# Windowed attention into a GEGLU feed-forward on one core: the first batch's loads, masks and order of work rearranged, and the second batch's attention moved into the first output stage

## The chip, the core and the metric

The kernel runs on one core of a Trainium2 chip. The core has a matrix engine (PE, which reads its stationary operand with separate weight loads, PEld), a vector engine (DVE), a scalar engine (ACT), a general-purpose engine (POOL) and SP, which here only issues transfers. Each engine works through its own list of instructions in order; they meet at semaphores. Transfers between main memory and the on-chip memory (SBUF) are issued from SP, ACT or POOL and are carried by 16 DMA engines. In this kernel the transfers that POOL issues for q, k, v and the weights convert 32-bit to 16-bit floating point on the way; they are called cast DMAs here. Matmul results go to PSUM, eight banks of 512 32-bit columns in each of 128 partitions.

The metric is the device time of one execution in microseconds (us). Lower is better.

## The reference, cut to what matters

```python
batch, n_heads, seq, head_dim = (8, 8, 576, 64)      # q, k, v, f32
window, dilation, scale = 32, 4, 1 / 8
rel = pos[:, None] - pos[None, :]
mask_plain = (rel >= 0) & (rel < window)
mask_dil = (rel >= 0) & (rel < window * dilation) & (rel % dilation == 0)
# heads 0-3 use mask_plain, heads 4-7 use mask_dil
attn = softmax(where(mask, scale * q @ k.T, -1e9))
x = (attn @ v).transpose(0, 2, 1, 3).reshape(4608, 512)
g, val = x @ w_gate, x @ w_val                        # 512 x 1536 each
out = (gelu(g) * val) @ w_out                         # 1536 x 512
```

Inputs and output are 32-bit; the kernel computes its matmuls in 16-bit floating point and accumulates in 32 bits.

## The kernel before, in words

**Attention.** Work is cut into pairs of heads, numbered n = 4 b + pair for batch b: two plain pairs and two dilated pairs in each batch (numbers 0 and 1 of batch 0 are plain, 2 and 3 dilated; 4 and 5 plain, 6 and 7 dilated for batch 1). A dilated head is treated as four residue classes of 144 positions, each with a plain window of 32. For each pair `emit_s` makes the scores of only those 128-key blocks that the window touches, in four PSUM banks, and ACT takes their exp into a tile `P`. The mask is applied in one of two ways: with `pe_mask`, a matmul of the identity with a bias of 0 or -60000 is accumulated ahead of the scores; without it, `emit_s` returns a function, called later, which multiplies `P` by a 0/1 mask on DVE (L383). `emit_pv` makes the denominators (`den`, a matmul with ones) and the numerators (`num`, a matmul with V). `norm_r` transposes the denominators out of PSUM into `dt` on DVE, and `recip` takes the reciprocal and transposes back, giving `rb`; `norm_x` multiplies the numerators by `rb` into `xT`, the transposed input of the feed-forward part. `b0` names the first PSUM bank that a step uses.

**Transposed q and k.** For batches 0 and 1 q and k are transposed by PE with an identity matrix. Plain heads come six rows to a partition (`sixes`, 96 partitions), are cast to 16 bits and transposed in `t_plain`; DVE or ACT copies the result out of PSUM into `qTp`. Dilated heads come four rows to a partition (`quads`): 128 partitions for the first 512 rows (`t_dil`) and 16 partitions for the last 64 rows (`t_rest`), copied into `qTd`. Later batches use transposes by DMA.

**Feed-forward.** Tokens go in nine chunks of 512. Per chunk c there are twelve blocks of 128 hidden columns: `ffn1` makes the gate and the value (4 matmuls each), `geglu` takes gelu on ACT (L584) and multiplies on DVE (L585) into `u_all`. Then `ffn2`, the output stage, makes four tiles of 128 tokens, twelve matmuls each (L596), and `store` copies each tile out and sends it away on SP. The first two blocks of chunks 0 and 1 are made together, one quarter of the contraction at a time (`ffn1_two`), so that they can begin when only the first quarter of `xT` is there.

**Order of the work.** The order is written out by hand: instructions stand on each engine in the order of the source. The front (L618 to L686) does batch 0: SP and ACT load plain q and k in 32 bits, then dilated q and k (L622 to L624), then V; POOL loads the identity and the masks from constants in main memory. DVE, ACT and POOL cast. Then scores, denominators and numerators of pairs 0 to 3 follow; pairs 2 and 3 use the banks of their forerunners (`emit_s(2, 0)`, `emit_s(3, 0)`). POOL issues gate and value weights of thirds 0, 1 and 2 by cast DMA (`load_w`, L654, L657, L658); thirds 0, 1, 2 serve blocks 0-3, 4-7, 8-11.

Behind the front (L689 to L708) stand the loads of batch 1: plain q and k on SP, held back until value weights 1 are there (`gate["dma"]`); dilated q and k, then output weights 0 on POOL; four casts of plain q and k; output weights 1 and 2; and then V of batch 1. Batch 1 is transposed between the blocks of chunk 0: a dilated group behind blocks 8 and 11, a plain group behind blocks 9 and 10 (L761 to L767). Output stage 0 (L787 to L799) makes its four tiles one after another, each with the full twelve matmuls, and the scores, denominators and numerators of pairs 4 to 7 are hung between these matmuls as hooks. Every later output stage does the same for the next batch with a list of places; that part is not touched.

Scratch: plain q and k of batch 0 land in the space of `u_all` (`first_p`), dilated q and k in the unused end of `xT` (`first_d`, `first_r`).

## Time and profile before

| | |
|---|---|
| median of 3 runs | 357.31 us (357.14 to 357.68) |
| the profiled execution | 357.14 us, with a span of 355.3 us from its first to its last instruction |
| mean granted clock of PE | 0.986 |
| first FFN matmul | 26.04 us after the start of the span |
| first output matmul | 50.47 us |
| first FFN matmul of chunk 1 | 68.05 us |
| gate weights 0 and value weights 0 issued | 15.84 and 16.61 us; they took 6.9 and 8.6 us to land |
| plain q and k of batch 1 issued | 31.08 and 31.45 us; cast by POOL from 38.96 to 44.3 us |

All times in a profile are counted from the start of the span. The page gives the busy time of each engine, the span in 40 slices of about 8.9 us with the granted clock of PE and the share of the DMA engines, the chain of work that ended last, and groups of like instructions. A table by stage can be asked for any stretch, and the instructions can be listed in order of time. A row of that list reads: start, length, engine, line of the source, operation, what it writes and reads, shape, how many were merged; in brackets the idle time of the engine before it and what ended that. Matmul ends are modelled; in a dense stream one of 512 columns starts every 0.215 us.

### The profile page before, as it was taken

How to read it: one execution, taken by the hardware profiler on the slowest of the kernel's cores; microseconds unless marked ns; L12 is line 12 of the kernel's file. 1: busy time of each engine (PE TensorE's matmuls, PEld its weight loads, DVE VectorE, ACT ScalarE, POOL GpSimd, SP SyncE). 2: the span in 40 equal slices, each digit the busy share in tenths (PEclk: the TensorE clock that was granted, in tenths of full speed). 3: DMA queues.
4: the chain of work that ended last, by engine and by line, in shares of the span. 5: the costliest groups of instructions: out<-in, count | busy, mean ns of one | idle time of the engine just before them, and what ended most of it. 6: DMA issues, size and time to landing. Idle time of an engine off the chain costs nothing.

```text
span 355.3 us, 5974 instructions
## 1 busy us (share of the span) xinstructions
PE 340.1 (96%) x2330; PEld 165.3 (47%) x2330; DVE 202.5 (57%) x313; ACT 146.6 (41%) x217; POOL 78.2 (22%) x110
## 2 busy tenths in 40 slices
PE   5789999999999999999999999999999999999995
PEld 2554454444454444444545454544454444444442
DVE  3575456743486348783778765985399423303420
ACT  2733255253553355535562447236733223323320
POOL 2680334550422350063004500240000000000000
PEclk9959999999999999999999999999999999999999
DMA  8999999999999898799149942792200020020002
GB/s 205 237 176 211 230 151 202 178 165 246 181 140 210 194 165 163 169 163 146 65 135 194 151 93 90 178 156 55 89 2 0 31 89 1 2 89 30 2 30 89
DMA packets 107292, 45.31 MB, mean 128 GB/s; under 512 B 83040, under 2 KB 102496, under 8 KB 107264
## 3 DMA queue, kind: packets, MB, share of 16 engines
q1 hardware_dynamic: 84272, 31.21, 39.5%
q0 software_dynamic: 21456, 12.01, 27.0%
q10 hardware_dynamic: 1536, 1.70, 2.1%
q8 instruction: 18, 0.29, 0.4%
q14 instruction: 10, 0.08, 0.1%
HBM read 40.13 MB, written 9.44 MB: 140 GB/s over the span
## 4 chain that ended last, share of the span: by engine, by line
PE 78%; DVE 13%; DMA 3%; issue 3%; ACT 2%; ACTq 0%; DVEq 0%
PE ps L562 46%; PE ps L596 22%; PE ps L455 5%; DMA xT<-in_k_dram 3%; DVE rb L522 2%; DVE dt L513 2%; DVE dt L483 2%; DVE u_all L585 2%; DVE xT L537 2%; DVE P L383 1%; PE ps L373 1%; DVE xT L493 1%; PE ps L343 1%; DVE rc L520 1%; PE ps L359 1%
## 5 line engine op out<-in xcount | busy, mean ns | idle before, releaser
L585 DVE SCALAR_TENSOR_TENSOR u_all<-g,ps 128x512 f16<-128x512 f16 x108 | 72.7, 683 | 76.8 <-PE ps L562 68.4
L562 PE MATMUL ps<-xT,wg 128*128 128x512 f16 x432 | 114.7, 381 | 0.6 <-DVE xT L534 0.2
L562 PE MATMUL ps<-xT,wv 128*128 128x512 f16 x432 | 114.3, 380 | 0.5 <-ACT osb L607 0.3
L584 ACT ACTIVATE g<-ps 128x512 f16<-128x512 f32 x108 | 63.8, 597 | 121.6 <-PE ps L562 121.5
L596 PE MATMUL ps<-wo,u_all 128*128 128x512 f16 x432 | 100.2, 380 | 0.0
L562 PEld LDWEIGHTS <-wv 128*128 128x128 f16 x432 | 42.4, 98 | 52.4 <-issue 2.5
L562 PEld LDWEIGHTS <-wg 128*128 128x128 f16 x432 | 41.3, 98 | 49.2 <-issue 2.5
L596 PEld LDWEIGHTS <-u_all 128*128 128x128 f16 x432 | 39.4, 98 | 45.2 <-issue 0.2
L607 ACT ACTIVATE osb<-ps 128x512 f32<-128x512 f32 x33 | 19.7, 598 | 38.1 <-PE ps L596 37.5
L199 POOL CAST qp<-st 128x2048 f16<-128x2048 f32 x6 | 11.4, 1894 | 97.6 <-DMA st<-in_k_dram 97.6
L513 DVE STREAM_TRANSPOSE dt<-ps 128x576 f32<-128x576 f32 x23 | 17.9, 779 | 15.4 <-PE ps L455 15.3
L522 DVE STREAM_TRANSPOSE rb<-rc 128x576 f32<-128x576 f32 (+4 forms) x34 | 25.3, 743 | 1.2
L375 ACT ACTIVATE P<-ps 128x1152 f16<-128x1152 f32 x16 | 18.1, 1130 | 18.5 <-PE ps L373 18.5
L353 ACT ACTIVATE P<-ps 128x960 f16<-128x960 f32 x16 | 15.5, 970 | 10.9 <-PE ps L343 10.8
L537 DVE TENSOR_TENSOR xT<-ps,rb 128x576 f16<-128x576 f32 x16 | 17.9, 1130 | 0.3
L609 DVE TENSOR_SCALAR osb<-ps 128x512 f32<-128x512 f32 x3 | 2.1, 691 | 27.8 <-PE ps L596 27.8
L455 PE MATMUL ps<-P,ones 128*64 128x96 f16 (+5 forms) x174 | 12.0, 251 | 4.3 <-DVE P L383 2.1
L383 DVE TENSOR_TENSOR P<-P,mask_p 128x1344 f16<-128x1344 f16 x14 | 12.5, 904 | 5.0 <-ACT P L354 4.9
L455 PEld LDWEIGHTS <-ones 128*64 128x64 f16 x174 | 7.8, 110 | 13.7 <-issue 11.0
L383 DVE TENSOR_TENSOR P<-P,mask_d 128x1152 f16<-128x1152 f16 x11 | 8.3, 757 | 10.2 <-ACT P L375 10.2
L483 DVE STREAM_TRANSPOSE dt<-ps 64x576 f32<-64x576 f32 x14 | 10.9, 781 | 0.4
L183 POOL CAST vp<-sv 128x1024 f16<-128x1024 f32 x8 | 8.5, 1059 | 12.0 <-DMA sv<-in_v_dram 12.0
(83 smaller groups left out, 242.3 us busy)
## 6 DMA issues: line engine op xcount, KB each, us to landing
out_dram<-osb SPq DMA_DIRECT2D x36, 256.0 KB, 2.0
sv<-in_v_dram SPq DMA_DIRECT2D x40, 128.0 KB, 3.9
st<-in_q_dram SPq DMA_DIRECT2D x24, 128.0 KB, 3.4
st<-in_k_dram SPq DMA_DIRECT2D x24, 128.0 KB, 3.0
qd<-in_q_dram POOLq DMA_DIRECT2D x7, 256.0 KB, 5.1
qd<-in_k_dram POOLq DMA_DIRECT2D x7, 256.0 KB, 6.5
vd<-in_v_dram POOLq DMA_DIRECT2D x7, 256.0 KB, 6.8
wg<-in_moe_w_gate_dram POOLq DMA_DIRECT2D x3, 512.0 KB, 7.9
```

What stands on the lines that cost most here:

```text
L375: nc.scalar.activation(pt, ps[:, b0 : b0 + 4, 0:DW], AF.Exp, bias=0.0, scale=scale)
L383: nc.vector.tensor_tensor(pt, pt, mb, ALU.mult)
L455: nc.tensor.matmul(o, lhs, rhs, start=st, stop=True, skip_group_check=True)
L483: nc.vector.transpose(dt[64 * hl : 64 * hl + 64].rearrange("p b c -> p (b c)"), both_rows(1 - hl, b0, hl))
L513: nc.vector.transpose(dst, den)
L522: nc.vector.transpose(rb[:, 0 : 32 * nb].rearrange("p (b c) -> p b c", c=32), bass.AP(tensor=rc.tensor, offset=rc.offset, ap=[rc.ap[0], [1 ...
L537: nc.vector.tensor_tensor(dst.rearrange("p (i m s) -> p i m s", m=2, s=2), num, rb.rearrange("p (s m i) -> p i m s", s=2, m=2), ALU.mult,)
L562: nc.tensor.matmul(ps[:, bank, :], w[:, kc, ns], xT[kc][:, tok], start=first, stop=end)
L584: nc.scalar.activation(g, ps[:, banks[0], :], AF.Gelu)
L585: nc.vector.scalar_tensor_tensor(u_all[:, nb, :], g, USCALE, ps[:, banks[1], :], ALU.mult, ALU.mult)
L596: nc.tensor.matmul(ps[:, bank, :], u_all[:, fc, tb * P : (tb + 1) * P], wo_t[fc // 4][:, fc % 4, :], start=(fc == 0), stop=(fc == NNB - 1),)
L607: nc.scalar.activation(osb, ps[:, bank, :], AF.Copy, bias=0.0, scale=1.0 / USCALE)
```

## The change

In the front:

- Dilated q and k of batch 0 are no longer loaded in 32 bits on SP and ACT. POOL issues them first of all, as cast DMAs, eight rows to a partition (`eights`, 72 partitions). `t_dil` now makes 16 transposes of 72 columns for each half and copies each group of four heads' classes in one piece; `t_rest`, its 32-bit identity and the four 32-bit tiles are gone.
- The identity and both masks are made on POOL with memsets and `affine_select` in place of being loaded. The bias of the plain mask is made on DVE at that place, ahead of the memsets of V and the casts of q; that of the dilated mask moves from POOL to DVE.
- 22 warm-up matmuls in place of 16.
- On POOL the cast of V stands ahead of the first gate and value weights; half of `last_keys` and the cast of dilated V follow before the other weights.
- Pairs 2 and 3 use different banks, so the scores of 3 do not wait for the exp of 2. The denominators of 0 and 1 are taken in a row into scratch of their own. The numerators of 0 and 1 are copied out by ACT and multiplied by POOL (`num_split`).

Behind the front:

- Plain q and k of batch 1 are held until gate weights 2 are there. Dilated q and k of batch 1 (as `eights`) and all of V go ahead of output weights 0 to 2; V's plain part is held until dilated k is there.
- The plain groups of batch 1 are transposed behind blocks 10 and 11, both dilated groups behind the last block. Then scores 4, 5 and 6 and the denominators and numerators of 4 come before any output matmul.
- Output stage 0 works by thirds: the four tiles accumulate in four banks (6, 7, 4, 5), four matmuls each per third, with the rest of the attention of batch 1 between the thirds. A one-column gelu stands at its end.

```diff
@@ front: helpers @@
-    first_d = [x32[t][:, 0 : HK * 4 * D] for t in range(2)]
-    first_r = [x32[2 + t][0:16, 0 : HK * 4 * D] for t in range(2)]
+    first_n = [x32[g][:, 0:S] for g in range(2)]
+    first_t = [x32[2 + g][:, 0:S] for g in range(2)]
+    def identity():
+        nc.gpsimd.memset(ident, 1.0)
+        for sign in (1, -1):
+            nc.gpsimd.affine_select(
+                out=ident, in_=ident, pattern=[[sign, P]], compare_op=ALU.is_ge, fill=0.0, base=0, channel_multiplier=-sign
+            )
+    def band(t, step, off):
+        for sign, base in ((1, off), (-1, WIN - 1 - off)):
+            nc.gpsimd.affine_select(
+                out=t,
+                in_=t,
+                pattern=[[sign * step, t.shape[1]], [sign, t.shape[2]]],
...
+    def mask_plain():
+        nc.gpsimd.memset(mask_p, 1.0)
+        band(mask_p[:, 0:PB].rearrange("p (r c) -> p r c", c=PW), 0, 0)
+        band(mask_p[:, PB : PB + P].rearrange("p (r c) -> p r c", r=1), 0, 0)
+        band(mask_p[:, PB + P : PH].rearrange("p (r c) -> p r c", r=1), 0, 64)
+        nc.vector.tensor_scalar(bias_p, mask_p, 1.0, 60000.0, ALU.subtract, ALU.mult)
+    def mask_dil():
+        nc.gpsimd.memset(mask_d, 1.0)
+        by_class = mask_d.rearrange("p (m i) -> p m i", m=2)
+        band(by_class[:, :, 0:P], 0, 0)
+        band(by_class[:, :, P:NCL], 64, 48)
+    def load_eights(b):
+        q8 = ldp.tile([R8, 2, HK, 8, D], F16, tag="qd", name=f"qd{b}")
+        for t, src in ((0, q), (1, k)):
+            tiles["last"] = nc.gpsimd.dma_start(
+                out=q8[:, t].rearrange("p h r d -> p h (r d)"), in_=eights(src, b, HK, H)
+            )
+        return q8
+    def t_dil(b, hp, q8, b0, engs):
+        qtd_ = tiles["qT", b][1]
+        for t in range(2):
             for hl in range(2):
+                for r in range(4):
+                    c0 = ((hl * 2 + r % 2) * 2 + r // 2) * R8
                     nc.tensor.transpose(
+                        ps16[:, b0 + t, c0 : c0 + R8],
+                        q8[:, t, 2 * hp + hl, 2 * r : 2 * r + 2, :].rearrange("p r d -> p (r d)"),
+                        ident[0:R8, 0:R8],
                     )
             copy(
                 engs[t],
+                qtd_[:, t, 2 * hp : 2 * hp + 2].rearrange("p h m (i u) -> p (h m) i u", u=2),
+                ps16[:, b0 + t, 0:S].rearrange("p (c u i) -> p c i u", c=4, u=2),
+            )
@@ front: order @@
-    nc.gpsimd.dma_start(ident, id_dram.ap())
-    nc.gpsimd.dma_start(mask_p, mp_dram.ap())
-    for t, src, eng in ((0, q, nc.sync), (1, k, nc.scalar)):
-        eng.dma_start(out=fh(first_d[t]), in_=quads(src, 0, HK, 0, 4 * P))
-        eng.dma_start(out=fh(first_r[t]), in_=quads(src, 0, HK, 4 * P, S))
-    nc.gpsimd.dma_start(ident32, id32_dram.ap())
-    nc.gpsimd.dma_start(mask_d, md_dram.ap())
+    qd0 = load_eights(0)
+    identity()
+    mask_plain()
+    mask_dil()
...
-    warm(16, 7)
+    warm(22, 7)
...
+    nc.vector.tensor_scalar(bias_d, mask_d, 1.0, 60000.0, ALU.subtract, ALU.mult)
     load_v_dil_rest(0)
+    v_cast(0, sv0)
     load_w(0)
-    v_cast(0, sv0)
-    copy("pool", tiles["v", 0][1], r4(first_vd))
-    w1 = load_w(1)
-    load_w(2)
...
+    def num_split(n, b0):
+        emit_pv(n, b0, ("num",))
+        rb = tiles.pop(("rb", n))
+        nc.scalar.copy(first_n[n], psf[:, b0 * 512 : b0 * 512 + S])
+        nc.gpsimd.tensor_tensor(xT[n][:, 0:S], first_n[n], rb, ALU.mult)
     emit_s(0, 4, pe_mask=True)
     emit_s(1, 0, pe_mask=True)
...
+    t_dil(0, 0, qd0, 4, ("dve", "dve"))
+    t_dil(0, 1, qd0, 6, ("act", "act"))
+    last_keys(0, 0, 2)
+    last_keys(0, 2, HK, nc.gpsimd)
+    copy("pool", tiles["v", 0][1], r4(first_vd))
+    load_w(1)
+    wg2, _ = load_w(2)
+    dt0, dt1 = (den(n, -2 * n, t.rearrange("p (b c) -> p b c", c=32)) for n, t in enumerate(first_t))
+    recip(0, dt0)
+    recip(1, dt1)
+    emit_s(2, 4, pe_mask=True)
     emit_s(3, 0, pe_mask=True)
...
+    den(2, 4)
+    num_split(0, 4)
+    num_split(1, 0)
+    emit_pv(2, 2, ("num",))
+    den(3, 4)
+    norm_x(2, 2)
+    num(3, 0)
-    gate["dma"] = w1
+    gate["dma"] = wg2
...
+    qd1 = load_eights(1)
+    gate["dma"] = tiles["last"]
+    v_plain(1, sv1, nc.sync)
+    load_v_dil(1)
+    for i in range(3):
+        gate["dma"] = load_wo(i)
@@ chunk 0 @@
-            if c == 0 and nb in (9, 10):
-                t_plain(1, q61, nb - 9, 4 + 2 * (nb - 9), ("act", "dve"))
-            if c == 0 and nb in (8, 11):
...
+            if c == 0 and nb > 9:
+                t_plain(1, q61, nb - 10, 4 + 2 * (nb - 10), ("act", "dve"))
...
         if c == 0:
             load_batch_rest(2)
-            ffn2(c, 0, 0, {5: [s_next]})
-            store(c, 0, 0, "act")
-            ffn2(c, 1, 1, {4: [s_next], 8: [lambda: md(4)]})
...
+            for hp in range(2):
+                t_dil(1, hp, qd1, 4 + 2 * hp, ("dve", "dve"))
+            outs = (6, 7, 4, 5)
+            def third(i, tbs):
+                for tb in tbs:
+                    ffn2(c, tb, outs[tb], fcs=range(4 * i, 4 * i + 4))
+                    if i == 2:
+                        store(c, tb, outs[tb], "act")
+            def both(n, b0):
+                emit_pv(n, b0)
+                norm_r(n, b0)
+                norm_x(n, b0)
+            masks.append(emit_s(4, 0))
+            masks.append(emit_s(5, 4))
+            mask_next()
+            emit_s(6, 0, pe_mask=True)
+            mask_next()
+            den(4, 4)
+            num(4, 4)
+            third(0, (0, 1))
+            emit_s(7, 0, pe_mask=True)
+            third(0, (2, 3))
+            both(5, 0)
+            third(1, (0, 1, 2, 3))
+            both(6, 0)
+            third(2, (0, 1, 2, 3))
+            both(7, 0)
+            gelu_table()
```

## The prediction

> **What bounds the kernel now.** I read the page's busy shares first, then the table by stage, then the order of time in the two places that the change touches. PE is busy in 340.1 of 355.3 us, so the first question is where it is not.
>
> ```profile
> PE 340.1 (96%) x2330; PEld 165.3 (47%) x2330; DVE 202.5 (57%) x313; ACT 146.6 (41%) x217; POOL 78.2 (22%) x110
> ...
> PEclk9959999999999999999999999999999999999999
> DMA  8999999999999898799149942792200020020002
> ```
>
> The reader is to see two things: PE is the bound on average, and the only slice with a lower granted clock (the 5) is the third, 18 to 27 us, in the front. The table by stage says the same; its columns are the length, busy us (and instructions) of PE, PEld, DVE, ACT and POOL, the granted clock, the DMA share and GB/s.
>
> ```profile
> 4.00:8.00 4.00, 2.43 (x11) 0.93 (x9) 0.36 (x1) 0.25 (x1) 0.00 (x0) 1.00 1.12 257
> 20.00:24.00 4.00, 3.34 (x36) 1.97 (x33) 2.69 (x5) 1.55 (x2) 4.00 (x6) 0.50 1.17 189
> 55.00:60.00 5.00, 4.36 (x36) 2.05 (x38) 3.28 (x5) 3.08 (x4) 1.99 (x3) 1.00 1.01 208
> ```
>
> Until 26.0 us, when the first FFN matmul starts, PE works with gaps and partly at half clock. From there to 74 us it idles only 0.64 us (before 59.8, in the last row) and about 0.3 us at 73.2. There is nothing to win in output stage 0: its attention work already lies between output matmuls. What can be won lies before 26 us; what can be lost lies in both. These rows, in order of time, price the rest:
>
> ```profile
> 7.64 1.02 DVE L266 CAST qp<-u_all 96x768 f16<-96x768 f32 x2 [4.19 <-DMA u_all<-in_q_dram]
> ...
> 8.59 0.42 PE L277 MATMUL ps<-ident,qp 96*128 96x96 f16 x6 [2.16 <-DMA ident<-attn_identity]
> ...
> 10.56 1.19 POOL L650 TENSOR_SCALAR bias_d<-mask_d 128x288 f16<-128x288 f16 x1 [7.01 <-DMA mask_d<-mask_dil]
> ...
> 18.16 1.04 POOL L183 CAST vp<-sv 128x1024 f16<-128x1024 f32 x1 [0.77 <-DMA sv<-in_v_dram]
> ...
> 26.93 2.12 DVE L537 TENSOR_TENSOR xT<-ps,rb 128x576 f16<-128x576 f32 x2
> ...
> 48.28 0.75 DVE L266 COPY qTp<-ps 128x576 f16<-128x576 f16 x1
> ...
> 50.51 0.75 DVE L266 COPY qTd<-ps 128x512 f16<-128x512 f16 x2
> ```
>
> See that the plain casts of batch 0 start at 7.64 us when q has landed, that sv lands at 18.16, that the last two products of batch 0 end at 29.05 us, and that a copy gathering 576 f16 columns with a stride costs 0.75 us where one of 512 in order costs 0.375.
>
> **The front, part by part.** The profiled execution took 357.14 us, 1.84 more than its span and 0.17 below the median. I call the delay of the plain casts behind 7.64 us d.
>
> *Dilated q and k on POOL's queue.* The same 1.18 MB now leaves at 1.2 us, beside plain q and k, not behind them. In 4 to 8 us the DMA share is already 1.12. At 4 us plain q and k have 0.69 MB to go and need 3.4 us more; no packet of POOL's queue moves before 4.0 us in the trace. If it takes a third of the engines, d grows by half of that, 1.7; bounds 0 (it takes nothing) and 3.4 (half the engines).
>
> *Masks made by POOL.* Behind two DMA issues (to 2.75 us) come three memsets and twelve selects, 2176 elements per partition, in place of four DMAs. Nothing in this trace is a select. POOL's casts (256 elements 0.41 us, 1024 in 1.04) give 0.82 ns an element and 0.2 us each; the TENSOR_SCALAR gives 4.1 ns. A select reads one stream and writes one, so it is nearer the casts; I take 1.5 ns. The identity is then ready at 3.8 us, the plain mask (memset 0.75, 1344 elements 2.0, six starts 1.2) at 7.8; by the casts 6.7, by TENSOR_SCALAR 10.4. On DVE the bias (0.34 us) now stands *ahead* of six V memsets (1.95) and the two casts of q; all wait for POOL. DVE is free for the casts at 10.1 (9.0 to 12.7). It ends later than the transfer (7.64 + 1.7), so d = 2.5, with 0.8 and 5.0 as ends.
> [...]
>
> *Clock.* Six more warm-up matmuls (0.215 us each at full clock) end at 7.7 us instead of 6.4, but the first transposes move from 8.6 to about 11, a longer gap than the 2.16 us shown. The trace loses its clock at 17.9 us, after a stretch of mostly transposes, and regains it at 28.1. If it falls earlier, plain scores cost up to 1.7 us more (bias matmuls 4 x 0.14, scores 0.3, twice); if not, 0. I take 0.8.
> [...]
>
> *Attention of batch 0, reordered.* From the second plain exp's end (14.07 + d) step by step: dilated copies 2 x 0.75 on DVE and 2 x 0.64 on ACT to 15.4; scores 2 (1.7 us at the half clock) 17.1, their exp 18.3; scores 3 need no exp any more and end at 18.8, exp 20.0; denominators 2 at 19.5; numerators 0, 1, 2 and denominators 3 on PE to 22.5; DVE transpose and reciprocal of 3 (1.9) to 24.4, two products of 1.06 to 26.5 + d. Before, this end was 29.05: the order saves 2.55. The two plain products go through an ACT copy (0.64) and POOL (at least 0.8 each by its casts), ready by 23.5 + d, ahead of need.
>
> *Weights.* On POOL the first weight issue now stands behind the V cast and so behind sv's landing. That transfer's issue no longer stretches over 12.2 us, so I put it at 15.8, with the casts of 1.5 the issues at 17.3 and 18.1 instead of 15.8 and 16.6. The uncontended output weights took 5.6 and 7.6 us to land, so value weights 0 are there at 25.7 (before 25.2). Each later megabyte follows 2.6 us on, before its block asks for it. This hides while PE starts at 25.7 or later; with sv 2 us later, 2 us are lost.
>
> Front: last data at 26.5 + 3.3 = 29.8, four matmuls end at about 30.9 with what is still cold ahead of them; before, those 16 ended at 30.5. **+0.4**, bounds -1.4 (start at 25.7, full clock) and +3.6 (d = 5.0 and 1.7).
>
> **Output stage 0.** T0 is the end of the last gate/value block. One plain transpose group (0.51) and one dilated group (0.74) leave the blocks, so T0 comes 1.25 earlier. After T0 on PE: 0.51 + 1.28 of transposes, scores 4 and 5 (0.8), 6 and 7 (1.92), values 4 to 7 (3.74), 48 output matmuls (10.3): 18.6 us of work, where before it was 18.4 from T0 to the next FFN matmul with 0.64 idle inside. But no output matmul lies ahead of the first value product:
> - DVE has the last geglu to T0 + 0.8, a plain copy to 1.5, four strided copies of 0.75 to 4.5, keys 0.3. Scores 5 write the banks that the copies read: PE, done with scores 4 at 2.4, waits some 2.0 us (and 0.35 earlier for a copy).
> - Output matmuls 0 write banks 6 and 7, where denominators 4 lie. DVE transposes these only behind mask 5 (exp 5 ends at 5.8, mask 0.9, transpose 0.8), at 7.6; PE is done at 6.8: 0.8 us.
> - Values 7 end at 21.8; DVE needs 0.8 + 1.1 + 1.06 to 25.0; 12 matmuls cover 2.6 to 24.4: 0.65 us.
> That is 18.6 + 3.8 = 22.4 against 18.4 and the 0.3 at 73.2, which the early gelu table takes away: 3.7 more, less the 1.25 that T0 gains: **+2.5.** With copies at 0.39 it is +1.0; with 3.4 us of it at half clock +4.2. I take the strided row, which has the same form.
> The new order of loads (batch 1 ahead of output weights) I cost at nothing: by thirds, the last output weights are asked for at about 65 us and at 2.6 us each land by 56. If plain q and k of batch 1, now gated on gate weights 2 (33.5 us) and not on value weights 1 (31.0), land 2 us late, at 44.3, their casts just meet block 10's end at 45 to 46; that cover gone costs up to 1. V of batch 1 (SP, behind dilated k at about 40) lands by 50, before its first use at 55; batch 2's loads, gated on output weights 2, start at 56 instead of 55.0, and its scores, first at about 89, have their transposes issued by 79.
>
> Sum: 357.14 + 0.4 + 2.5 = **360.0**; 360.2 against the median, which I give.
>
> **Rivals.**
> - *Slower still, 364* (361.8 to 366): selects at 4.1 ns (front +3.6 at most), or the clock falling in stage 0 (+1.7 for one 3.4 us window of output matmuls). For it: 7 us of transposes and small matmuls without a dense one. Against: the last such stretch held its clock for 9 us.
> - *Faster, 355.7*: sv lands at 13.5, so value weights 0 at 23.4, selects as cheap as casts, and the front keeps full clock, so 16 matmuls from 23.4 end at 26.9: -3.6; with stage 0 at +2.0, 357.3 - 1.6. For it: SP's queue holds half as much ahead of sv. Against: sv moves in packets under 512 B (1574 of them in 12 to 16 us), and the front's DMA share is already over 1. It decides where those 16 end before 28.0.
> - *No difference, 357.3*: the saved 2.55 comes through and the stage's loss is the low +1.0.
>
> **How the numbers follow.** Forecast 0.48 (own range 358.2 to 361.7), slower still 0.25, faster 0.20, no difference 0.07. Within 0.2% (0.7 us) is about what a measurement here can tell from nothing. Slower 0.73, same 0.07, faster 0.20. The range takes half of the faster case and most of the slow one: 355.8 to 364.5.
>
> **What would show it.** Right: DVE idle on the mask to 7 or 8 us; first FFN matmul at 25.5 to 27; after the last block four DVE copies of 0.75 with PE idle about 2 us, and no stall at the gelu table. Wrong: a select under 0.3 us with FFN matmuls dense by 23 to 24, or ordered-copy prices for the 576-column copies; a dip of the granted clock behind 45 us would be the first rival.

## The result and the profile after

The changed kernel takes 363.31 us (median of 4 runs, 363.00 to 364.37) against 357.5 for the kernel before beside it: a ratio of 1.0169 (95% interval 1.0145 to 1.0192), some 6 us slower. One execution of a later run, 398 us at a granted clock of 0.844, was in a slower state of the chip and is in no figure here. The profiled execution took 363.00 us with a span of 361.3, where that of before had 357.14 and 355.3.

The lines of the page of the changed kernel that answer to those shown of before:

```profile
PE 340.0 (94%) x2348; PEld 164.6 (46%) x2348; DVE 202.0 (56%) x307; ACT 147.8 (41%) x219; POOL 81.9 (23%) x121
...
PEclk9889998999999999999999999999999999999999
DMA  8999997999999992389528961793100020011002
```

PE is as busy as before (340.0 and 340.1 us), so in sum all 6 us are idle time of PE. Matmuls that a half clock stretches count as busy (below, eight take 3.56 us and the next eight 1.90): there are fewer of them in the front than before (the clock was 0.50 there from 18 to 28 us, here from 12 to 14 and from 25 to 28), and some in output stage 0, where there were none (1.00 from 30 to 74 us). The granted clock has its dips in slices 2, 3 and 7 (9 to 27 us and 54 to 63 us). The last is new. The table by stage, with the same columns as before:

```profile
4.00:8.00 4.00, 3.85 (x17) 1.52 (x15) 0.88 (x2) 0.00 (x0) 3.59 (x10) 1.00 1.13 252
...
12.00:16.00 4.00, 3.90 (x58) 2.69 (x57) 1.06 (x4) 2.56 (x4) 0.00 (x0) 0.67 1.15 177
16.00:20.00 4.00, 2.81 (x46) 1.82 (x45) 3.92 (x7) 2.35 (x4) 3.59 (x6) 1.00 0.17 14
20.00:24.00 4.00, 2.18 (x56) 1.84 (x53) 3.84 (x7) 3.58 (x4) 4.00 (x6) 1.00 1.19 189
...
56.00:60.00 4.00, 1.57 (x13) 0.81 (x14) 2.26 (x4) 0.00 (x0) 2.66 (x4) 0.88 0.58 132
60.00:64.00 4.00, 4.00 (x26) 1.75 (x25) 0.00 (x0) 0.58 (x1) 1.20 (x3) 0.70 1.15 156
```

and one row of the kernel before:

```profile
56.00:60.00 4.00, 3.36 (x32) 1.71 (x33) 3.28 (x4) 2.11 (x3) 1.99 (x3) 1.00 0.93 192
```

Two rows matter. From 56 to 60 us PE works 1.57 of 4 us, where before it worked 3.36, and the clock falls behind that, from 59.0 to 62.4 us. From 16 to 20 us the DMA engines stand nearly still (share 0.17), since the first weights are now issued behind the V cast, at 17.73 us. The rows of the front and of the stage in order of time (start, us, engine, line, operation):

```profile
4.64 2.39 POOL L113 TENSOR_SCALAR_AFFINE_SELECT mask_p<-mask_p 128x480 f16<-128x480 f16 x6
...
7.06 0.44 DVE L128 TENSOR_SCALAR bias_p<-mask_p 128x672 f16<-128x672 f16 x1 [5.59 <-POOL mask_p L113]
...
9.47 0.99 DVE L290 CAST qp<-u_all 96x768 f16<-96x768 f32 x2
...
23.53 2.80 POOL L673 TENSOR_TENSOR xT<-xT,rb 128x576 f16<-128x576 f32 x2
...
24.28 2.13 DVE L548 TENSOR_TENSOR xT<-ps,rb 128x576 f16<-128x576 f32 x2
25.02 0.58 PE L573 MATMUL ps<-xT,wg 128*128 128x512 f16 x1 [2.08 <-POOL xT L673]
...
30.33 1.03 PE L573 MATMUL ps<-xT,wg 128*128 128x512 f16 x4
...
46.94 0.43 PE L301 MATMUL ps<-ident,qp 96*128 96x96 f16 x6 [0.64 <-POOL qp L288]
...
50.47 2.74 DVE L290 COPY qTd<-ps 128x576 f16<-128x576 f16 x4
...
52.60 0.37 PE L349 MATMUL ps<-qTp 64*128 64x160 f16 x6 [1.10 <-DVE qTd L290]
...
57.34 1.04 POOL L199 CAST vp<-sv 128x1024 f16<-128x1024 f32 x1 [8.92 <-DMA sv<-in_v_dram]
58.43 0.45 PE L461 MATMUL ps<-P,vp 128*64 128x160 f16 x8 [3.03 <-POOL vp L199]
...
58.93 3.56 PE L607 MATMUL ps<-wo,u_all 128*128 128x512 f16 x8
...
63.31 1.90 PE L607 MATMUL ps<-wo,u_all 128*128 128x512 f16 x8
...
74.26 0.39 PE L573 MATMUL ps<-xT,wg 128*128 128x512 f16 x1
```

The front is done at the time of before: its first 16 FFN matmuls end at 30.33 us (before 30.5). The last block ends at 48.93 (49.64), so 0.71 us is gained there. From there to the first FFN matmul of chunk 1 it takes 25.33 us (18.41): 6.92 us are lost in output stage 0, and the difference is still 6.58 at a wait for masks that both traces have further on (134.97 and 141.55). The spans differ by 6.0, so the rest of the changed kernel is 0.6 us shorter.

In the stage PE waits 1.10 and 0.29 us for strided copies, 0.45 for an exp, and then **3.03 us for V of batch 1**, which POOL can cast only at 57.34. Behind this wait eight output matmuls take 3.56 us where the next eight take 1.90.

V is not later than in the kernel before. There its cast and its first use are:

```profile
58.01 1.04 POOL L183 CAST vp<-sv 128x1024 f16<-128x1024 f32 x1 [10.26 <-DMA sv<-in_v_dram]
...
64.20 0.43 PE L455 MATMUL ps<-P,vp 128*64 128x160 f16 x8
```

In the new order PE has nothing else to do from 55.4 us on, nine us before the old first use, and the new order of loads brings the cast only 0.67 us forward.

### The profile page after: what moved, and what is told of

Same layout as the page of the kernel before. It is cut to its first block, busy times and chain, and to the rows that moved or that the text cites. A ratio compares the mean times of both kernels' runs of the same rounds, so it can differ in the third digit from the quotient of the medians.

```text
span 361.3 us, 6016 instructions
## 1 busy us (share of the span) xinstructions
PE 340.0 (94%) x2348; PEld 164.6 (46%) x2348; DVE 202.0 (56%) x307; ACT 147.8 (41%) x219; POOL 81.9 (23%) x121
## 4 chain that ended last, share of the span: by engine, by line
PE 68%; DVE 12%; DMA 11%; issue 3%; POOL 3%; SPq 1%; ACT 1%; DVEq 0%; POOLq 0%; ACTq 0%
PE ps L573 39%; PE ps L607 22%; DMA sv<-in_v_dram 7%; DMA qd<-in_k_dram 5%; PE ps L461 4%; DVE xT L548 2%; DVE dt L489 2%; DVE u_all L596 2%; DVE rb L533 2%; DVE dt L522 2%; DVE xT L499 1%; DVE P L389 1%; SPq L195 1%; PE ps L379 1%; DVE rc L531 1%
## 5 line engine op out<-in xcount | busy, mean ns | idle before, releaser
L607 PEld LDWEIGHTS <-u_all 128*128 128x128 f16 x432 | 40.2, 99 | 46.9 <-issue 1.6
L522 DVE STREAM_TRANSPOSE dt<-ps 128x576 f32<-128x576 f32 x21 | 16.3, 777 | 20.6 <-PE ps L461 20.4
L389 DVE TENSOR_TENSOR P<-P,mask_d 128x1152 f16<-128x1152 f16 x11 | 8.4, 761 | 10.2 <-ACT P L381 10.2
```

What stands on the lines that cost most here:

```text
L389: nc.vector.tensor_tensor(pt, pt, mb, ALU.mult)
L522: nc.vector.transpose(dst, den)
L607: nc.tensor.matmul(ps[:, bank, :], u_all[:, fc, tb * P : (tb + 1) * P], wo_t[fc // 4][:, fc % 4, :], start=(fc == 0), stop=(fc == NNB - 1),)
```

## The experiments

My theory after the result: V of batch 1 is late, because its issue on SP's queue waits for dilated k of batch 1 and then shares the engines with three output weights that POOL issued between 32.6 and 38.5 us; it landed at 57.2, and the half clock follows from the wait. Rivals: the strided copies and the chain scores, exp, mask, denominators that now lies ahead of the first output matmul; the half clock by itself; the changed front.

**V no longer gated.**

```diff
-    gate["dma"] = tiles["last"]
     v_plain(1, sv1, nc.sync)
```

> The changed kernel with one wait less: plain V of batch 1 goes out on SP right behind plain q and k, not held until dilated k has landed. Three theories stand for the 6 us that the changed kernel is over the one before. Late V: PE's 3.0 us wait of numerators 4 for the V cast, and the half clock behind it, are the larger part; then V is cast by about 52 us, that wait shrinks to under 0.8 us (the rest of denominators 4's transpose), and the time falls by 2.2 us if the clock still falls, by 4.2 us if it holds: 359.0 to 361.2. Concentration: scores, masks and values of batch 1 ahead of the output matmuls cost it whatever V does, since the DVE chain of mask and transposes takes the place of V's wait: at most 0.7 us less, 362.6 or more. Front: nothing less, 363.3.

Measured: 362.65 us, ratio 1.015 (1.0133 to 1.0167). The gate was not the cause: the five issues of V began 8 us earlier, but took 12.7 us in place of 7.2, the cast began only 0.5 us sooner, at 56.80, and PE still waited.

```profile
35.60 12.67 SPq L195 DMA_DIRECT2D sv<-in_v_dram  x5
...
57.89 0.72 PE L461 MATMUL ps<-P,vp 128*64 128x160 f16 x8 [1.72 <-POOL vp L199]
58.79 0.27 PE L461 MATMUL ps<-P,vt 128*64 128x64 f16 x2 [0.18 <-POOL vt L203]
58.98 3.13 PE L607 MATMUL ps<-wo,u_all 128*128 128x512 f16 x8
```

So this run did not yet test what an early V is worth. Its clock is 0.67 already from 54 to 56 us, ahead of the wait.

**Unread matmuls into the wait for V.**

```diff
             den(4, 4)
+            for _ in range(30):
+                nc.tensor.matmul(ps[:, 3, 288:512], ones[:, 0:P], ones[:, 0:224], start=True, stop=True)
             num(4, 4)
```

> The changed kernel with 30 matmuls of 224 columns, whose result nobody reads, between denominators 4 and numerators 4 on PE, where it now waits 3.0 us for V; at 0.095 us each they take 2.9 us of that wait. V still comes as late. If the wait is what lets the clock fall, it stays up and the first eight output matmuls (3.35 us now, 1.72 at full clock) and scores 7 run at full speed: 1.9 us less, 361.4. If the clock falls for another reason (the transposes before it), or if its fall is hidden by a later wait, nothing is less: 363.3.

Measured: 364.2 us (ratio 1.0203, 1.016 to 1.0246). The fillers took 4.76 us, mostly at half clock (0.50 from 58 to 62 us), longer than the wait; the clock was 0.53 in 56 to 58 us, before they began at 59.37. The eight output matmuls behind them ran in 1.90 us. What they saved they cost, and the profiled execution was the longest of the four (366.85 us), with a wait of 2.03 us for the cast of plain k and half clock behind it already in block 10 (0.72 from 48 to 51 us). So the price stays undecided. In this trace and the last the clock fell ahead of the place of the wait for V, so it can fall without it; whether it would have in the changed kernel, where it fell behind the wait, is open.

**The changed front with the old loads and stage, and the old front with the new rest.** The first takes the code ahead of the loads of batch 1 from the changed kernel and all behind it from the kernel before, save that dilated q and k of batch 1 are still loaded eight rows to a partition (`eights`); the second is the reverse, so both have these loads. The core of the first:

```diff
-    gate["dma"] = wg2
+    gate["dma"] = w1
...
     qd1 = load_eights(1)
-    gate["dma"] = tiles["last"]
-    v_plain(1, sv1, nc.sync)
-    load_v_dil(1)
-    for i in range(3):
-        gate["dma"] = load_wo(i)
+    load_wo(0)
...
+    wo1 = load_wo(1)
+    wo2 = load_wo(2)
+    gate["dma"] = wo1
+    v_plain(1, sv1, nc.sync)
+    load_v_dil(1)
...
+            if c == 0 and nb in (8, 11):
+                t_dil(1, nb // 11, qd1, 6 - 2 * (nb // 11), ("dve", "act"))
```

> The front of the changed kernel with the loads of batch 1, the places of its transposes and the output stage 0 of the kernel before (dilated q and k of batch 1 still eight rows to a partition; no early gelu). By the two traces the front moves the end of the first 16 FFN matmuls by -0.2 us, so late V and concentration both expect 357.2, within 0.5 of the kernel before. The front theory (its POOL order and transfers hurt what follows) expects 359 or more.

> The front of the kernel before with all the rest of the change: loads of batch 1 in the new order, transposes behind the last blocks, output stage 0 by thirds, early gelu. Late V and concentration expect nearly the whole loss, 362.8 to 363.8; the front theory expects 359 or less.

Measured: front alone 359.4 (ratio 1.0058, 1.004 to 1.0076), rest alone 363.77 (1.0184, 1.0163 to 1.0205). The rest alone costs as much as the whole change. The two do not add: 2.2 and 6.5 over the kernel before are more than the 5.8 of both. In the front-only run the 16 matmuls end at 30.48 as in the kernel before, and the loss comes 12 us later, at block 8:

```profile
45.12 0.43 PE L319 MATMUL ps<-ident,qd 72*128 72x72 f16 x8 [2.13 <-DMA qd<-in_k_dram]
45.39 1.56 PE L573 MATMUL ps<-xT,wg 128*128 128x512 f16 x4
```

Dilated k of batch 1 is issued at 26.88 (before 24.12), since POOL's two products of batch 0 (2.79 us) stand ahead of it, it lands 2.5 us later, and half clock follows (0.72 from 44 to 48 us, 0.81 to 51). The products need not be the whole of it: a run below with the old front and the `eights` loads waits here too, 1.27 us. In the rest-only run the wait for V is 0.25 us, yet the stage takes 23.5 us; there the clock is 0.50 from 54 to 58 us. Its mask wait further on comes 2.1 us sooner than in the changed kernel (139.43), but what follows is longer by 1.4 in this execution, so little of it shows in its time.

**V ahead of the output weights.** Two edits to the changed kernel: no gate on V, and output weights 1 and 2 issued behind the casts of plain q and k on POOL.

```diff
-    gate["dma"] = tiles["last"]
     v_plain(1, sv1, nc.sync)
     load_v_dil(1)
-    for i in range(3):
-        gate["dma"] = load_wo(i)
+    load_wo(0)
...
             cast_six("pool", q61, st1, t, hp)
+    load_wo(1)
+    gate["dma"] = load_wo(2)
     v_cast(1, sv1)
```

> In the run that let V of batch 1 go without waiting for dilated k, V still landed at 56.8 us, because output weights 0 to 2 of POOL's queue shared the engines with it, so the time stayed (362.7); that run did not test late V. Here output weights 1 and 2 are issued behind POOL's casts of plain q and k (about 48 us), as in the kernel before, and V is not held. Late V: V is cast by 52 us, PE's wait ahead of numerators 4 falls from 3.0 to at most 0.8 us; 2 to 2.5 us less than the changed kernel, 360.8 to 361.4; output weights 1 and 2 land by 58 us, before they are asked for. Concentration with the clock: the run with the old front had a wait for V of 0.25 us only and still took 363.8, so what counts is PE idle and at half clock between the last block and the first third; here then 362.5 or more.

Measured: 360.91 us (1.009, 1.0061 to 1.0118). This time V is early: its issues begin at 35.53, as in the run without the gate, but the cast is at 52.03, and there is no wait for it:

```profile
55.65 0.77 PE L461 MATMUL ps<-P,ones 128*64 128x512 f16 x6 [0.45 <-ACT P L360]
56.18 0.75 PE L461 MATMUL ps<-P,vp 128*64 128x160 f16 x8
...
57.30 2.60 PE L607 MATMUL ps<-wo,u_all 128*128 128x512 f16 x8 [0.32 <-DVE dt L522]
```

The late V, with what follows from it, costs 2.4 us of the 6. The run without the gate differs from this one only in the place of output weights 1 and 2, so it was these beside V that made it late.

**The same with the dilated transposes back in blocks 9 and 10; and these transposes alone, with V still late.**

```diff
-                t_plain(1, q61, nb - 10, 4 + 2 * (nb - 10), ("act", "dve"))
+                t_plain(1, q61, nb - 10, 4, ("act", "dve"))
+            if c == 0 and nb in (9, 10):
+                t_dil(1, nb - 9, qd1, 6, ("dve", "act"))
...
-            for hp in range(2):
-                t_dil(1, hp, qd1, 4 + 2 * hp, ("dve", "dve"))
```

> As the run beside it (V first), and the two dilated transposes of batch 1 back between the blocks, behind blocks 9 and 10, their copies shared by DVE and ACT. This takes away scores 5's wait for the copies (1.1 + 0.3 us in the changed kernel's trace) and 1.3 us of transposes behind the last block, which moves ahead of it. Concentration: 1.4 us less than the run beside it, and if the clock holds for having fewer transposes in a row, up to 3.5 less. Late V: no change beyond 0.3, as mask and denominators come later anyway. A wait for dilated k at block 9 would eat the gain.

> Only the two dilated transpose groups go back from output stage 0 into blocks 9 and 10 of the changed kernel; V of batch 1 still comes as late as before. If the late V is the gate of the stage, what the groups save is eaten by a longer wait for it: the numerators of head 4 still start at about 58.3 us, the wait for V grows from 3.0 to 4 to 5 us, and the time is 362.9 to 363.6. If the two costs simply add, the time falls by the 1.3 us that the same move saved with V early: 361.8 to 362.2.

Measured: with V early 359.63 us (1.0065, 1.0047 to 1.0084), 1.3 less than without (the executions of the two overlap, 359.4 to 360.7 and 359.4 to 361.6; in the profiled ones chunk 1 begins 1.2 us sooner, at 70.44 and not 71.64); with V late 363.75 (1.0177, 1.0159 to 1.0195), nothing less than the changed kernel. With V late the numerators of head 4 begin at 58.82, where the changed kernel has 58.43, and wait 1.69 us for the cast (not the 4 to 5 I had put down: the cast of plain k holds block 10 up by 1.36 us and eats the rest). So the costs overlap: here the late V hid what else was late ahead of it, and undoing that part alone showed nothing.

**Does the half clock cost anything?** The version of 359.6 runs at half clock from 53.1 to 56.6 us. Unread matmuls were put into its waits, first 4 ahead of scores 5 and 11 ahead of scores 6, in a bank of scores 4, then 12 between scores 4 and 5 in another bank:

```diff
             masks.append(emit_s(4, 0))
+            for _ in range(12):
+                nc.tensor.matmul(ps[:, 7, 288:512], ones[:, 0:P], ones[:, 0:224], start=True, stop=True)
             masks.append(emit_s(5, 4))
```

> The version with V ahead of the output weights and the dilated groups in the blocks (359.6), with 15 matmuls of 224 columns, whose result nobody reads, put into waits of the stage: 4 ahead of scores 5, 11 ahead of scores 6, where PE waited 0.41 and 1.20 us. At full clock they take 0.1 us each and fit the waits. If the half clock from 53 to 56.6 us comes from a PE too idle from 50 to 53, the clock stays at 1.00, the bias matmuls, scores 6, denominators and numerators of head 4 take 1.2 us less, and the time falls by 0.5 to 1.3: 358.3 to 359.1. If the chain of exp, mask and denominators sets the end whatever the clock, 359.4 to 360.0.

> The version with V ahead of the output weights and the dilated groups in the blocks (359.6), with 12 unread matmuls of 224 columns between scores 4 and scores 5, in a bank that no exp reads (the fillers before stood in a bank of scores 4 and waited 2.46 us for its exp). PE has about 2 us of waits between the end of scores 4 and the bias matmuls of scores 6, the fillers take 1.2. If the half clock from 53 to 56.6 us follows from an idle PE from 50 to 53, it is gone here: bias matmuls of scores 6 in 0.65 and not 1.26 us, and the time falls by 0.4 to 1.2, to 358.4 to 359.2. If it stays, the time is 359.4 to 360.4.

The first was a bad test: the fillers waited 2.46 us for the exp that reads their bank, the clock fell all the same (0.50 from 56 to 58 us), and the time was 362.08 (1.0125, 1.0097 to 1.0154). The second held the clock, 1.00 in every window from 46 to 62 us, and took 359.98 us (1.0057, 1.0038 to 1.0075): no gain over 359.63. Its rows:

```profile
53.75 0.91 PE L365 MATMUL ps<-bias_d,ident 128*128 128x288 f16 x4 [0.42 <-ACT P L359]
...
55.38 0.45 PE L461 MATMUL ps<-P,ones 128*64 128x512 f16 x5 [0.35 <-ACT P L360]
...
56.97 1.89 PE L607 MATMUL ps<-wo,u_all 128*128 128x512 f16 x8 [0.81 <-DVE dt L522]
```

At full clock PE is done earlier and waits longer (0.81 us in place of 0.32) for DVE's transpose of the denominators; the first output matmul starts at 56.97, at half clock at 56.81. Counted from the end of the last block (49.98 and 49.61) that is 6.99 and 7.20 us. Here the chain scores, exp, mask, denominators, DVE sets the start, and the clock costs 0.2 us by the traces and nothing that the times show. What it costs in the changed kernel itself, where the first third ran at half clock behind the wait for V, was not separated.

**The weights first, in both stages.** The pause of the DMA engines from 16 to 19 us (share 0.08, then 0.00) suggested issuing weights 0 ahead of the V cast of batch 0; the second run also takes the old stage and the early gelu table.

```diff
-    v_cast(0, sv0)
     load_w(0)
+    v_cast(0, sv0)
```

> The changed kernel with gate and value weights 0 issued ahead of the V cast on POOL, as in the kernel before. In the changed kernel the DMA engines stand nearly still from 16 to 19 us (share 0.08 to 0.30), because these weights wait behind the V cast. If the POOL order of the front costs, all later transfers come 2 to 3 us earlier: first FFN matmul at 23 to 24 us, dilated k and V of batch 1 earlier by as much, 2 to 3.5 us less: 360 to 361.3. If it does not, or if V of batch 0 is delayed by the weights beside it, no change: 363.3, within 0.7.

> The run of the front alone (359.4) lost its time at block 8, where PE waited 2.1 us for dilated k of batch 1 (landed at 45.0) and then ran at half clock. Here the same front issues gate and value weights 0 ahead of the V cast, and output stage 0, as in the kernel before, ends with the early gelu. If the hole in the DMA engines' work at 16 to 19 us is the cause, dilated k lands at 42 to 43, the wait is under 0.5 us, and the front itself gains 1 to 2: 354.5 to 356.5, faster than the kernel before. If not: 359.

Measured: 364.41 (1.0205, 1.0181 to 1.023) and 359.78 (1.0059, 1.0039 to 1.0078). The weights took the engines from V of batch 0: its cast came at 19.06 and not 16.41, POOL's copy of the last keys stands behind it, PE waited 5.06 us for that copy, and the first FFN matmul started at 28.43. In the second the first 16 FFN matmuls end at 33.28, 2.8 us later than in the front-only run, yet the time is about the same: of the front-only run's wait of 2.13 us at block 8, 0.40 is left.

**The front's price in the old stage.** Four kernels with the changed front, the `eights` loads and the old stage, dilated transposes in blocks 10 and 11, where their data have landed: as it is; with the early gelu table; with that and the first gate weights issued ahead of the V cast, gated on the fourth block of V; and with output weights 0 held until the second gate weights have landed.

```diff
-            if c == 0 and nb in (8, 11):
-                t_dil(1, nb // 11, qd1, 6 - 2 * (nb // 11), ("dve", "act"))
+            if c == 0 and nb > 9:
+                t_dil(1, nb - 10, qd1, 4 + 2 * (nb - 10), ("dve", "act"))
```

> Front of the changed kernel, loads and output stage of the kernel before, and the transposes of dilated q and k of batch 1 moved from blocks 8 and 11 to blocks 10 and 11, behind the plain ones. If the 2 us that this front lost with the old stage were only the wait for dilated k at block 8 (landed 45.0, asked for at 42.9) and the half clock behind it, the wait is gone, granted clock 1.00 from 30 to 55 us, and since 64 short transposes replace 32 long ones and 32 of 16 rows, the last block ends some 0.6 us earlier: 356.6 to 357.4, no slower than before. If the front itself costs time, 359.0 to 360.0 as with the old blocks.

> The same with the one-column gelu at the end of output stage 0. The activation table is then loaded under the stage's last output matmuls and not ahead of the first gelu of chunk 1: 0.2 to 0.4 us less than the same kernel without it (356.3 to 357.1), if that stall was on the path; the same time if another wait ends at the same point.

> The front of the changed kernel with the old stage, late dilated groups and early gelu (360.6), where PE waited 0.62 and 2.11 us for output weights 1 and 2. Here the first gate weights are issued ahead of the V cast of batch 0, gated on the fourth block of that V, so that the transfers start some 1.4 us earlier into the 3 us in which the DMA engines stood still (16 to 19 us); nothing else moves. If this pause is what makes the output weights late, they land 1.3 to 1.5 us earlier, the waits fall from 2.7 to 1.3 us and the time to 359.0 to 359.6. If the lateness comes from POOL's order of issues alone, the waits stay at 2.5 to 2.8 and the time at 360.2 to 361.0.

> The front of the changed kernel with the old stage, late dilated groups and early gelu (360.6 and in a second look, with weights ahead, 359.5), and output weights 0 held on POOL until the second gate weights have landed. If the lateness of output weights 1 and 2 (2.7 us of waits) comes from output weights 0 ahead of plain k of batch 1, they are issued at 44.5 to 45.5 us and the time falls to 357.5 to 358.5. If plain k is late because the whole queue behind the POOL products of batch 0 is (dilated q and k issued 2.7 us later than before), it stays at 359 to 361.

Measured: about 361 (1.0084, 1.006 to 1.0108), 360.6 (1.0073, 1.0049 to 1.0098), 359.5 (1.0058, 1.0037 to 1.0079) and 360.1 (1.0085, 1.0057 to 1.0112); each spreads over 2.4 to 3.6 us, between 358.5 and 362.1. I expected 357 of the first, and that was wrong: the wait for dilated k is gone, and another has come. In the second:

```profile
52.17 0.38 PE L607 MATMUL ps<-wo,u_all 128*128 128x512 f16 x1 [0.62 <-DMA wo<-in_moe_w_out_dram]
...
55.81 0.38 PE L607 MATMUL ps<-wo,u_all 128*128 128x512 f16 x1 [2.11 <-DMA wo<-in_moe_w_out_dram]
```

The issue of output weights 1 and 2 stands on POOL behind the casts of plain q and k, and these wait for plain k. It lands 2.4 us later than in the kernel before:

```profile
44.36 2.37 POOL L288 CAST qp<-st 96x768 f16<-96x768 f32 x3 [3.50 <-DMA st<-in_k_dram]
46.67 1.49 POOL L145 DMA_DIRECT2D wo<-in_moe_w_out_dram  x2
```

Filling part of the pause left these two lines and the waits as they were (46.85, 0.58 + 2.15 us), and so did holding output weights 0 by 1.1 us (47.04, 0.55 + 2.25). That the time of the third is an us under the second's lies within their spread. So neither the pause nor, with this front, the place of output weights 0 makes plain k late. All that POOL issues for batch 1 stands some 2.8 us later, behind the products of batch 0, but the next runs show that this is not the whole reason either.

**Parts of the change on the kernel before.** Short transposes of dilated q and k of batch 1 and the early gelu table; then the same with the groups in blocks 10 and 11 and output weights 0 held until the second gate weights have landed.

```diff
-    qd1, rd1 = load_qk_dil(1)
+    qd1 = load_eights(1)
...
+            gelu_table()
```

> The kernel before, with two pieces of the change alone: dilated q and k of batch 1 loaded eight rows to a partition and transposed by 64 short transposes in blocks 8 and 11 (in place of 32 long and 32 of 16 rows, 0.83 us a block), and the one-column gelu at the end of output stage 0. The short groups take 0.52 us, so the stage begins 0.6 us earlier, and the wait of 0.3 us ahead of chunk 1 is gone: 356.4 to 356.9 if nothing else waits. If the strided copies of 0.75 us or a later landing of dilated k at block 8 take it back, 357.2 to 358.5.

> The kernel before with short transposes of dilated q and k of batch 1 and the early gelu table, as in the run that came out at 358.5, and two waits of that run mended. There output weights 0 were issued at 24.7 us, 4 us sooner than in the kernel before, took from plain k of batch 1, whose casts hold up the issue of output weights 1 and 2 on POOL (46.8 and not 44.3 us): PE waited 1.3 us for them. Here output weights 0 wait on POOL for the second gate weights, as they happened to do in the kernel before (28.7 us), and the dilated groups stand in blocks 10 and 11, where dilated k (1.27 us late at block 8) has landed. If the order of loads was the only cost, output weights 1 and 2 are issued at 44 to 45 us, no wait is left and the time is 356.3 to 357.0, under both kernels. If the casts still wait for plain k to 46 us or later, 358 to 359.

Measured: 358.53 (1.0024, 1.0005 to 1.0043) and 359.24 (1.0069, 1.0045 to 1.0093). In the first PE waits 1.27 us for dilated k at block 8 and 1.29 for output weights:

```profile
44.46 2.37 POOL L277 CAST qp<-st 96x768 f16<-96x768 f32 x3 [2.88 <-DMA st<-in_k_dram]
46.76 1.51 POOL L134 DMA_DIRECT2D wo<-in_moe_w_out_dram  x2
```

Plain k and output weights 1 and 2 are as late as in the kernels above (46.67 to 47.04 for the weights), and this front has no products on POOL. So the products are not needed for that; what is common is the `eights` loads and, but for the last of the four, earlier output weights 0. In the second, whose profiled execution was one of its shortest (357.97 us), 0.33 for output weights and 0.73 for a mask are left, and others take up to 361.3; what they wait for was not seen.

This second kernel and the last of the four above differ in the front alone. Output weights 1 and 2 are issued here (first line) and there (second) at:

```profile
45.40 1.51 POOL L134 DMA_DIRECT2D wo<-in_moe_w_out_dram  x2
...
47.04 1.50 POOL L145 DMA_DIRECT2D wo<-in_moe_w_out_dram  x2
```

At like loads the changed front makes them 1.6 us later, and the kernel 0.8 us slower by the medians (359.24 and 360.08), which is less than either spreads; the traces are of one of the shortest executions of the one and of the longest of the other. The rest of what the four cost over the kernel before they share with a kernel that has the old front. No version that I ran is faster than the kernel before.

## Why the prediction was right or wrong

The sign and the place were right: nothing from the front, a loss in output stage 0. The size was not: 2.9 us forecast, 5.8 measured.

- *Front, +0.4 forecast:* −0.2. Right within its bounds, but its inner terms were off and cancelled. The six selects of the plain mask cost 2.39 us, near the casts' price (2.3 by 0.82 ns an element and 0.2 us each); DVE was free at 9.47, where the prediction took 10.1; the end that it had by the casts was nearer, 9.0. The POOL transfer delayed plain k by 0.24 us, not 1.7. The last data came at 26.4, not 29.8. The upper bound should read +3.8 by its own terms (0.4 + 2.5 + 0.9).
- *The clock falls earlier in the front:* yes in the profiled execution, 0.61 from 11 to 12 us and 0.67 from 12 to 16, behind two us (8 to 10) without a matmul and the 24 transposes from 10.0 us on. The trace does not tell whether the pause or the transposes brought it, and it did not come each time: in the run of 364.41 (weights 0 ahead of the V cast), with a pause of 1.91 us in place of 2.16 and the same 24 transposes from 10.02 on, the clock was 1.00 from 8 to 20 us. In the changed kernel the fall stretched the plain scores and their bias matmuls by 1.5 us in sum. What that cost was not separated, since PE waited for POOL at the end of the front.
- *"The two plain products go through an ACT copy and POOL (at least 0.8 each by its casts), ready by 23.5 + d, ahead of need":* wrong. They cost 1.40 each, and PE waited 2.08 us for the first. They also push POOL's next issues by 2.8 us (26.24 against 23.39), which the prediction did not count. How much of the changed front's cost in the old stage comes from this stays open; by the two kernels that differ in the front alone, the front costs 0.8 us, not clear of their spread.
- *T0 1.25 earlier:* 0.71, and 0.17 of that is the front's. Plain q and k did land later, by 4.1 us and not 2 (their casts start at 43.00 and 46.05 us in place of 38.96 and 41.97), the cover that the prediction named was gone, and a wait of 0.64 for plain k's cast was left ("costs up to 1").
- *Waits at the strided copies, 2.35:* 1.39; the copies were 0.69 each, near the 0.75 taken. *Mask 5, 0.8:* hidden behind the wait for V (0.32 in the version with V first); 0.45 for an exp ahead of denominators 4 stands in its place. Right in kind, high by 1.3 together. *Values 7, 0.65:* 0.55. *Gelu stall gone:* yes.
- *"V of batch 1 (SP, behind dilated k at about 40) lands by 50, before its first use at 55":* the step that failed, and with it the new order of loads, costed "at nothing" with a reason given for the output weights and batch 2 but not for what they do to V. Dilated k landed at 43.6; V, held until then, was issued behind all three output weights and not ahead of them. Its five issues took 7.2 us (the shortest 0.39), and the last of its data landed at 57.2, up to 12.1 us after its issue. PE waited 3.03 us; with output weights 1 and 2 behind V the time falls by 2.4.
- *The rival "slower still", by the clock in stage 0:* the fall came, from 59.0 to 62.4 us, and stretched the first third by 1.66 us (3.56 against 1.90). The rival, like the +4.2 for the stage, had put down 1.7 us for 3.4 us of it; no row of before shows that length (its one fall lasted 10.2 us, 17.9 to 28.1), but it is what the changed kernel shows. Its condition was met and I had given it 0.25. What it costs in the changed kernel no run separated; in the version where the clock was held it was 0.2 us by the traces. That the rival's 364 lies next to the measured 363.3 is in part luck: the late V, the larger term, is not in it.

From T0 to chunk 1 the forecast was 21.75 us (22.4 less the 0.65 of values 7, which falls inside chunk 1), the trace has 25.33: +3.03 for V, +1.66 for the clock, −1.3 for the waits over-priced, and 0.2 that is left over. By the runs: 363.3 less 2.4 (V first) less 1.3 (dilated transposes in the blocks, with V first) is 359.6. The last 2.2 us no run took away: in the trace with the clock held PE waits 0.44, 0.42, 0.35 and 0.81 us along the chain ahead of the first output matmul, where the old stage has output matmuls to do. That these waits are the 2.2 us is argued from the trace, not shown.

## What to carry to other kernels

Before an attention chain is put ahead of the matmuls that used to cover it, ask when each of its inputs lands in the *new* order of loads: here five transfers issued beside three output weights of another queue took 7.6 to 12.1 us each to land in place of 6.1 to 6.5. Costs that wait for the same late transfer need not add: undo them in order of lateness, the last first, or an experiment may show nothing, as here. Instructions moved onto a queue that also issues transfers delayed these too, by 2.8 us for 2.8 us of work here. And before a cost is put down to one of several changes by exclusion, look for a run without that change: here one had the same late transfers.

## What was not expected of the hardware

- Loads of V in 256-byte rows from SP's queue took long beside converting transfers of POOL's queue. In the changed kernel the five issues stretch over 7.2 us, and the cast, which waits for the data, comes 13.7 us after the first of them; issued 8 us earlier the issues took 12.7 us and the cast came 21.2 us after the first, with output weights 1 and 2 behind them 10.5 and 16.5; the kernel before has 4.9 and 8.1, and 6.1 to 6.5 us to landing. The issues of that tile in the changed kernel:

```profile
L195 SPq DMA_DIRECT2D sv<-in_v_dram x5: 385/501/3201, 43.7 to 47.6; - x5
...
DMA to landing us min/median/max: 7.6/10.4/12.1
```

- The clock fell in output stage 0 behind stretches in which PE idled: in the changed kernel at 59.0 us, behind 3.0 us without a matmul; in the version of 359.6 at 53.1, where PE was busy 1.16 of 2 us from 50 to 52 and 0.17 of the next. There 12 dense matmuls (1.32 us) between scores 4 and 5 were enough to hold it in the profiled execution (1.00 from 46 to 62 us).
- A load of the kernel before just met its use and shows no wait: dilated k of batch 1 landed at 42.6 us for a block at 42.59. Every version with other loads was slower by its median (the nearest by 0.24%), and several spread over more than 3 us, where the kernel before stays within 2.6.
